# Key loads of 48-KB rows in two places, values two or three chunks behind, in a decode attention kernel

## Chip, cores, metric

One core of a Trainium2 chip; the other cores are idle. The metric is the device time of one execution in microseconds. A "span" is what the profile of one execution covers; it is 1.7 to 1.9 us shorter than the time of that execution in most kernels here (more in three, see e7).

## The reference

One decode step: layer norm of one row, attention with 32 heads over a cache of 32768 keys and values of 192 numbers each, output projection, residual, then a small dense block. Cut to what matters:

```python
B, Sq, D = 1, 1, 640
H, Sk, Dh = 32, 32768, 192
q = (layernorm(x) @ wq).reshape(B, Sq, H, Dh).transpose(0, 2, 1, 3)
scores = jnp.einsum("bhqd,bhkd->bhqk", q, k_cache) * (Dh ** -0.5)
p = softmax(scores, axis=-1)
o = jnp.einsum("bhqk,bhkd->bhqd", p, v_cache)
h = x + o.transpose(0, 2, 1, 3).reshape(B, Sq, H * Dh) @ wo
# ... h2 = h + relu(layernorm(h) @ w1) @ w2
```

Keys and values are 805 MB in bf16, each read once. All inputs together are 825 MB.

## The kernel before

In this kernel each engine has its own program, and semaphores tie them. A head's keys come in four loads of 128 partitions x 64 keys (a row of 24 KB for each partition), its values likewise. A load is worked off in two chunks of 32 keys per partition. In each chunk PE transposes a part of the keys and multiplies it with the query, DVE does the rest by multiply and reduce, ACT takes the exponentials, and PE sums the values with them.

```python
kt = [sbuf(f"kt{i}", [P, JL * Dh], bf16, 512) for i in range(NL)]   # 4 key places of 24 KB
vt = [sbuf(f"vt{i}", [P, JL * Dh], bf16, 512) for i in range(NV)]   # 2 value places of 24 KB
# ... the issuing queue (cut):
for h in range(H):
    for ld in range(NL if h < LAST else NL - 1):
        n = NL * h + ld
        load(kt[ld][:], rows(k_hd, h, P * JL * ld, JL), f"dk{ld}", "k", h, ld)
        if n >= NV:
            hp, lp = divmod(n - NV, NL)
            g.wait("PV", hp, 2 * lp + 1)          # PE has summed what lay in this value place
        load(vt[ld % NV][:], rows(v_hd, h, P * JL * ld, JL), f"dv{ld % NV}", "v", h, ld)
# ... PE, one head (cut):
for c in range(NC):
    transposes(g, h, c)
    if c > 0:
        values(g, h, c - 1)                       # values one chunk behind
    elif h > 0:
        values(g, h - 1, NC - 1)
        den_mm(g, h - 1)
    scores_pe(g, h, c)
```

The end of the last head has its own loads: keys of 40, 16 and 8 per partition, their values, then the two weights of the dense block.

The softmax here doesn't subtract the row's maximum and nothing guards it: scores larger than these inputs give would overflow.

## Time and profile before

| | |
|---|---|
| time, median | 1924.24 us (1924.01 to 1924.29, 3 runs) |
| span of the profiled run | 1922.4 us |
| bytes moved | 825.26 MB in 44793 packets |
| rate in the middle | 432 to 433 GB/s |
| PE, DVE busy | 81%, 81% |

The rows of the page with 40 figures cut the span into 40 slices: busy tenths for an engine, GB/s for the transfers. The chain of waits follows the work that ended last backwards; where it consists of transfers (76% of the span here), they were what the work waited for. A landing time counts from the issue of a load to its last byte: a key load that lands 22.5 us after its issue, three times the 7.28 us of its own transfer, is taken to have had two others ahead of it. The prediction shows these lines.

### The profile page before, as it was taken

The numbers are of one execution on the slowest core, as the hardware profiler recorded it, in microseconds if no ns is written. First come the engines' busy times: TensorE is split into PE (matmuls) and PEld (weight loads), VectorE is DVE, ScalarE is ACT, GpSimd is POOL, SyncE is SP. The second block draws the span as 40 slices with busy tenths as digits, with TensorE's granted clock in tenths as the row PEclk, the third lists the DMA queues.
The fourth block names the chain that finished last, engine by engine and source line by source line (L and its number), as shares of the span: only waits on it lengthen the run. The fifth ranks groups of instructions, "written<-read, shape, count | busy, mean of one in ns | idle before, by whom it ended". The sixth has DMA issues, their size and how long they took to land.

```text
span 1922.4 us, 36522 instructions
## 1 busy us (share of the span) xinstructions
PE 1563.5 (81%) x15899; PEld 1073.1 (56%) x15899; DVE 1560.6 (81%) x734; ACT 970.7 (50%) x2031; POOL 0.7 (0%) x6
## 2 busy tenths in 40 slices
PE   5888888788888888788787888888878887888887
PEld 4555555555555555555555555555545555555555
DVE  5878888887887888787888878888778887888886
ACT  3555455454555555454454555545445454555554
POOL 0000000000000000000000000000000000000000
PEclk9898888988888898888898888888888888898888
DMA  9999999999999999999999999999999999999998
GB/s 405 430 431 432 432 434 433 433 431 432 433 431 433 434 433 432 432 432 428 435 434 433 432 432 433 433 432 432 432 433 433 432 433 433 432 433 433 433 430 342
DMA packets 44793, 825.26 MB, mean 429 GB/s; under 512 B 4580, under 2 KB 6116, under 8 KB 12132
## 3 DMA queue, kind: packets, MB, share of 16 engines
q1 hardware_dynamic: 44762, 824.99, 99.9%
q8 instruction: 12, 0.20, 0.0%
q14 instruction: 9, 0.07, 0.0%
q10 hardware_dynamic: 10, 0.00, 0.0%
HBM read 824.97 MB, written 0.00 MB: 429 GB/s over the span
## 4 chain that ended last, share of the span: by engine, by line
DMA 76%; PE 21%; SPq 2%; issue 1%; ACT 0%; POOLq 0%; DVE 0%
DMA kt<-in_A_k_cache_dram 76%; PE o_ps L324 11%; PE tp L343 10%; SPq L224 2%; PE sp L324 0%; PE attT L324 0%; ACT kT L538 0%; POOLq L306 0%; PE mm L324 0%; DVE o_pair L638 0%; ACT pB L544 0%; PE mm L527 0%; DVE y_row L713 0%; ACT h1T L600 0%; DVE oT L648 0%
## 5 line engine op out<-in xcount | busy, mean ns | idle before, releaser
L623 DVE TENSOR_TENSOR pr<-kt,qb 128x2304 f32<-128x2304 bf16 (+2 forms) x257 | 756.0, 2942 | 278.9 <-POOLq L290 261.5
L538 ACT COPY kT<-tp 128x1024 bf16<-128x1024 bf16 (+1 forms) x899 | 818.8, 992 | 319.3 <-PE tp L343 317.3
L343 PE MATMUL tp<-ident_f,kt 128*128 128x128 f32 x3459 | 569.7, 331 | 334.3 <-POOLq L306 334.3
L626 DVE TENSOR_REDUCE sc<-pr 128x12 f32<-128x2304 f32 (+2 forms) x257 | 755.3, 2939 | 8.9
L343 PEld LDWEIGHTS tp<-ident_f,kt 128*128 128x128 f32 x3459 | 496.1, 172 | 351.3 <-POOLq L306 350.1
L324 PE MATMUL o_ps<-vt,pB 128*2 128x384 bf16 x2286 | 472.5, 358 | 6.8 <-POOLq L306 6.6
L324 PE MATMUL o_ps<-vt,pA 128*2 128x384 bf16 x1778 | 331.0, 326 | 0.0
L324 PEld LDWEIGHTS o_ps<-vt,pB 128*2 128x2 bf16 x2286 | 184.5, 89 | 244.7 <-issue 88.3
L544 ACT ACTIVATE pB<-sp 128x20 bf16<-128x20 f32 (+2 forms) x258 | 47.9, 186 | 504.5 <-PE sp L324 504.5
L324 PEld LDWEIGHTS sp<-qm,kT 128*128 128x128 bf16 x6918 | 193.3, 97 | 77.9 <-issue 65.2
L324 PEld LDWEIGHTS o_ps<-vt,pA 128*2 128x2 bf16 x1778 | 150.7, 85 | 144.9 <-issue 7.9
L324 PE MATMUL sp<-qm,kT 128*128 128x2 bf16 x6918 | 212.0, 164 | 3.1 <-ACT kT L538 2.4
L553 ACT ACTIVATE pA<-sc 128x12 bf16<-128x12 f32 (+2 forms) x257 | 53.4, 208 | 106.4 <-DVEq L65 104.7
L544 ACT ACTIVATION_READ_ACCUMULATOR pB<-sp 128x1 f32 x258 | 50.2, 195 | 0.0
L553 ACT ACTIVATION_READ_ACCUMULATOR pA<-sc 128x1 f32 x257 | 48.7, 190 | 0.0
L631 DVE TENSOR_REDUCE rec<-mm 128x1 f32<-128x20 f32 x32 | 5.7, 179 | 50.3 <-PE mm L324 49.8
L324 PE MATMUL mm<-wq_s,xn_ln 128*1 (+1 forms) x160 | 18.7, 248 | 4.0 <-POOLq L306 4.0
L638 DVE TENSOR_SCALAR o_pair<-o_ps,rec 2x384 bf16<-2x384 f32 x32 | 19.4, 605 | 2.7 <-PE o_ps L324 1.7
L324 PE MATMUL attT<-oT,wo_s 128*128 128x1 bf16 x465 | 15.9, 163 | 0.3 <-DVE oT L648 0.3
L324 PEld LDWEIGHTS mm<-dsums,ones_mat 128*128 128x128 f32 x64 | 9.5, 188 | 10.7 <-issue 9.3
L324 PEld LDWEIGHTS attT<-oT,wo_s 128*128 128x128 bf16 x465 | 13.8, 96 | 0.4 <-DVE oT L648 0.4
L324 PE MATMUL mm<-ones_row,row_e 1*128 1x1 bf16 x384 | 14.0, 159 | 0.0
(71 smaller groups left out, 144.9 us busy)
## 6 DMA issues: line engine op xcount, KB each, us to landing
kt<-in_A_k_cache_dram SPq DMA_DIRECT2D x127, 3072.0 KB, 22.5
vt<-in_A_v_cache_dram SPq DMA_DIRECT2D x127, 3072.0 KB, 15.6
wq_s<-in_A_wq_dram SPq DMA_DIRECT2D x4, 1920.0 KB, 21.0
wo_s<-in_A_wo_dram SPq DMA_DIRECT2D x16, 480.0 KB, 16.3
kt<-in_A_k_cache_dram SPq DMA_DIRECT2D x1, 1920.0 KB, 20.2
kt<-in_A_v_cache_dram SPq DMA_DIRECT2D x2, 960.0 KB, 24.8
kt<-in_B_w_dram SPq DMA_DIRECT2D x1, 1920.0 KB, 18.5
wq_s<-in_B_w_dram SPq DMA_DIRECT2D x1, 960.0 KB, 20.5
```

The lines of the kernel that those rows point to most:

```text
L224: g.do(lambda: nc.sync.dma_start(out=dst, in_=src), sem, label, by=16)
L324: return lambda: pe.matmul(o, lhsT=w, rhs=r, **kw)
L343: calls.append(lambda b=b, o=o: pe.transpose(out=dst[:, b, :], in_=src[:, o:o + 2 * P].bitcast(f32), identity=ident_f[:]))
L538: g.do(lambda: act.copy(out=kT[c % 2][:, b0:b0 + nb, :], in_=src[:, 0:nb, :].bitcast(bf16)), "act_pe", ("cp", h, c, k))
L544: g.do(lambda: act.activation(out=pB[c % 4][:, 0:jp], in_=sp[:, 0:jp], func=F.Exp, scale=SCALE, accum_out=dsums[:, 2 * c + 1:2 * c + 2]), ...
L553: g.do(lambda: act.activation(out=pA[c % 4][:, 0:jd], in_=sc[c % NC][:, 0:jd], func=F.Exp, scale=SCALE, accum_out=dsums[:, 2 * c:2 * c + 1 ...
L623: g.chain(lambda: dve.tensor_tensor(out=pr[:, 0:j1 - j0, :], in0=src[:, (off + j0) * Dh:(off + j1) * Dh].rearrange("p (j d) -> p j d", d=D ...
L626: g.chain(lambda: dve.reduce_sum(out=sc[c % NC][:, j0:j1], in_=pr[:, 0:j1 - j0, :], axis=X), "dve")
L631: g.chain(lambda: dve.reduce_sum(out=rec[:, 0:1], in_=mm[:, 0:2 * NCM], axis=X), "dve")
L638: g.do(lambda: dve.tensor_scalar_mul(out=o_pair[:, :, 1, :], in0=o_ps[0:2, 0:2 * Dh].rearrange("q (i d) -> q i d", i=2), scalar1=rec[0:2, ...
```

## The change

The intent is larger rows: for all heads but the last, two key loads of 128 keys per partition (48-KB rows) into two places, instead of four of 64 into four. Values stay at 24-KB rows. As four chunks can start only when a whole key load is there, values come two or three chunks behind the scores (one in the kernel before), and the order of the loads is key 0, old value 3, value 0, key 1, value 1, value 2. In the last head the keys lead their values. The core of the diff:

```diff
-    kt = [sbuf(f"kt{i}", [P, JL * Dh], bf16, 512) for i in range(NL)]
+    kt = [sbuf(f"kt{i}", [P, JK * Dh], bf16, 512) for i in range(NK)]
...
+        def keys(h, ld):
+            if h > 0:
+                g.wait("PV", h - 1, 4 * ld + 1)
+                g.wait("scs", h - 1, 4 * ld + 3)
+            load(kt[ld][:], rows(k_hd, h, P * JK * ld, JK), f"dk{ld}", "k", h, ld)
+
+        def vals(h, ld):
+            if ld == 1 and h > 0:
+                g.wait("PV", h, 0)
+            elif ld > 1:
+                g.wait("PV", h, 2 * ld - 3)
+            elif h > 0:
+                g.wait("PV", h - 1, 5)
...
+    SUMS = ((), (-2,), (-1,), (0, 1), (), (2,), (3,), (4, 5))
     def pe_head(g, h, turn=None):
         for c in range(NC):
             transposes(g, h, c)
-            if c > 0:
-                values(g, h, c - 1)
...
+            for d in SUMS[c]:
+                if d >= 0:
+                    values(g, h, d)
+                elif h > 0:
+                    values(g, h - 1, NC + d)
             scores_pe(g, h, c)
...
     def pe_end(g):
...
+        transposes(g, h, 6)
+        values(g, h, 3)
+        for c in (7, 8, 9):
             transposes(g, h, c)
+            if c > 7:
+                values(g, h, c - 4)
             scores_pe(g, h, c - 1)
-            if c > E0 + 1:
-                values(g, h, c - 2)
```

More of the change, by code (lines that the diff above doesn't have):

```diff
@@ L106 @@
     FT = Dff // P
+    JK = 128
     JL = 64
@@ L110 @@
     QG = 8
+    NK = Sk // (P * JK)
     NL = Sk // (P * JL)
@@ L114 @@
     LAST = H - 1
-    assert Sk % (P * JL) == 0 and NL == 4 and 2 * Dh == 3 * P and H % QG == 0 and H % 2 == 0 and H >= 4
-    full = [(c // 2, (c % 2) * J, J, JPS[c % 2]) for c in range(NC)]
+    assert Sk % (P * JK) == 0 and NK == 2 and NL == 4 and 2 * Dh == 3 * P and H % QG == 0 and H % 2 == 0 and H >= 4
+    full = [(c // 4, (c % 4) * J, J, JPS[c % 2], c // 2, (c % 2) * J) for c in range(NC)]
     ENDJ = (40, 16, 8)
-    ends = full[:NC - 2] + [(NL - 1, 0, 20, 12), (NL - 1, 20, 20, 12), (NL, 0, 16, 8), (NL + 1, 0, 8, 8)]
+    ends = [(c // 2, (c % 2) * J, J, JPS[c % 2]) for c in range(NC - 2)]
+    ends += [(NL - 1, 0, 20, 12), (NL - 1, 20, 20, 12), (NL, 0, 16, 8), (NL + 1, 0, 8, 8)]
+    ends = [q + q[0:2] for q in ends]
     assert sum(ENDJ) == JL
@@ L195 @@
     wq_v = wq_s[:].rearrange("p (c n) -> p c n", c=DT)
-    k_at = {(LAST, NL - 1): kt[3][:, 0:40 * Dh],
-            (LAST, NL): kt[0][:, 40 * Dh:56 * Dh], (LAST, NL + 1): kt[0][:, 56 * Dh:64 * Dh]}
-    v_at = {(LAST, NL - 1): kt[0][:, 0:40 * Dh],
-            (LAST, NL): kt[1][:, 0:16 * Dh], (LAST, NL + 1): kt[1][:, 16 * Dh:24 * Dh]}
-    w1_s = kt[1][:, 24 * Dh:24 * Dh + DT * Dff].rearrange("p (c n) -> p c n", n=Dff)
+    k_at = {0: kt[0][:, 0:64 * Dh], 1: kt[0][:, 64 * Dh:128 * Dh], 2: kt[1][:, 0:64 * Dh],
+            3: kt[1][:, 64 * Dh:104 * Dh], 4: kt[1][:, 104 * Dh:120 * Dh], 5: kt[1][:, 120 * Dh:128 * Dh]}
+    v_at = {3: kt[0][:, 0:40 * Dh], 4: kt[0][:, 40 * Dh:56 * Dh], 5: kt[0][:, 56 * Dh:64 * Dh]}
+    w1_s = kt[0][:, 64 * Dh:64 * Dh + DT * Dff].rearrange("p (c n) -> p c n", n=Dff)
     w2_s = wq_s[:, 0:FT * D].rearrange("p (f n) -> p f n", n=D)
-    assert 24 * Dh + DT * Dff <= JL * Dh and FT * D <= DT * QG * Dh
+    assert DT * Dff <= JL * Dh and FT * D <= DT * QG * Dh
     W2_CUTS = (0, FT // 2, FT - 2, FT)
     def k_tile(h, ld):
-        return k_at[(h, ld)] if (h, ld) in k_at else kt[ld][:]
+        return k_at[ld] if h == LAST else kt[ld][:]
     def v_tile(h, ld):
-        return v_at[(h, ld)] if (h, ld) in v_at else vt[ld % NV][:]
-    names = ["pool_pe", "act_pe", "dve_pe", "act_dve", "dve_act", "dve", "dve_row", "pe_dve", "pool_row", "pool_dve", "pool_act", "pe_act", "pe"]
-    names += [f"dk{i}" for i in range(NL)] + [f"dv{i}" for i in range(NV)] + ["dwq", "dwo", "dx", "dout"]
-    names += [f"dke{i}" for i in range(2)] + [f"dve{i}" for i in range(4)] + ["dw1"] + [f"dw2_{i}" for i in range(3)]
+        return v_at[ld] if h == LAST and ld in v_at else vt[ld % NV][:]
+    names = ["pool_pe", "act_pe", "dve_pe", "act_dve", "dve_act", "dve", "dve_row", "pe_dve", "pool_row", "pool_dve", "pool_act", "pe_act", "pe", "dve_sp"]
+    names += [f"dk{i}" for i in range(NK)] + [f"dv{i}" for i in range(NV)] + ["dwq", "dwo", "dx", "dout"]
+    names += [f"dke{i}" for i in range(4)] + [f"dve{i}" for i in range(4)] + ["dw1"] + [f"dw2_{i}" for i in range(3)]
     sems = {n: nc.alloc_semaphore(n) for n in names}
@@ L227, in rows @@
             return src[h, k0:k0 + P * jl, :].rearrange("(p j) d -> p (j d)", p=P)
-        load(wq_v, wq_view[:, :, 0:QG * Dh], "dwq", "wq", 0)
-        for h in range(H):
-            for ld in range(NL if h < LAST else NL - 1):
-                n = NL * h + ld
-                load(kt[ld][:], rows(k_hd, h, P * JL * ld, JL), f"dk{ld}", "k", h, ld)
-                if n >= NV:
-                    hp, lp = divmod(n - NV, NL)
-                    g.wait("PV", hp, 2 * lp + 1)
-                load(vt[ld % NV][:], rows(v_hd, h, P * JL * ld, JL), f"dv{ld % NV}", "v", h, ld)
-                if ld == 0 and h % QG == QG - 1 and h + 1 < H:
-                    gq = (h + 1) // QG
-                    g.wait("PV", h - 1, 5)
-                    load(wq_v, wq_view[:, :, gq * QG * Dh:(gq + 1) * QG * Dh], "dwq", "wq", gq)
-                if ld == 3 and h % 2 == 0:
-                    if h > 0:
-                        g.wait("prj", h)
-                    load(wo_s[:], wo_view[h // 2], "dwo", "wo", h // 2)
+        def keys(h, ld):
[3 more added lines that the diff above has]
+            load(kt[ld][:], rows(k_hd, h, P * JK * ld, JK), f"dk{ld}", "k", h, ld)
@@ new lines, in vals @@
+        def vals(h, ld):
[5 more added lines that the diff above has]
+                g.wait("PV", h - 1, 5)
+            if h < LAST:
+                src = rows(v_hd, h, P * JK * (ld // 2), JK)[:, (ld % 2) * JL * Dh:(ld % 2 + 1) * JL * Dh]
+            else:
+                src = rows(v_hd, h, P * JL * ld, JL)
+            load(vt[ld % NV][:], src, f"dv{ld % NV}", "v", h, ld)
@@ new lines, in dma_program @@
+        load(wq_v, wq_view[:, :, 0:QG * Dh], "dwq", "wq", 0)
+        for h in range(LAST):
+            keys(h, 0)
+            if h > 0:
+                vals(h - 1, NL - 1)
+            vals(h, 0)
+            if h % QG == QG - 1:
+                gq = (h + 1) // QG
+                g.wait("PV", h - 1, 3)
+                load(wq_v, wq_view[:, :, gq * QG * Dh:(gq + 1) * QG * Dh], "dwq", "wq", gq)
+            keys(h, 1)
+            vals(h, 1)
+            vals(h, 2)
+            if h % 2 == 0:
+                if h > 0:
+                    g.wait("prj", h)
+                load(wo_s[:], wo_view[h // 2], "dwo", "wo", h // 2)
@@ L247, in dma_program, with end_keys @@
+        def end_keys(i, k0, jl, sem):
+            load(k_at[i], rows(k_hd, LAST, k0, jl), sem, "k", LAST, i)
+        for ld in range(NL - 1):
+            if ld != 1:
+                g.wait("PV", LAST - 1, 2 * ld + 1)
+                g.wait("scs", LAST - 1, 2 * ld + 3)
+            end_keys(ld, P * JL * ld, JL, ("dk0", "dke0", "dk1")[ld])
+            if ld == 0:
+                vals(LAST - 1, NL - 1)
+            else:
+                vals(LAST, ld - 1)
         k0 = P * JL * (NL - 1)
@@ L250, in dma_program @@
             at.append((k0, jl))
-            if i == 0:
-                g.wait("PV", LAST - 1, NC - 1)
-            else:
-                g.wait("PV", LAST, 1)
-            load(k_tile(LAST, NL - 1 + i), rows(k_hd, LAST, k0, jl), f"dk{NL - 1}" if i == 0 else f"dke{i - 1}",
-                 "k", LAST, NL - 1 + i)
+            end_keys(NL - 1 + i, k0, jl, f"dke{1 + i}")
             k0 += P * jl
+        vals(LAST, NL - 2)
         i = 0
         for ld, (k0, jl) in enumerate(at):
-            for c, (l, off, jc, jp) in enumerate(ends):
+            for c, (l, off, jc, *_) in enumerate(ends):
                 if l == NL - 1 + ld:
-                    if ld > 0:
-                        g.wait("PV", LAST, 3)
+                    g.wait("PV", LAST, 1)
                     load(v_tile(LAST, l)[:, off * Dh:(off + jc) * Dh],
@@ L266, in dma_program @@
                     i += 1
+        g.wait("PV", LAST, 3)
         load(w1_s, B_w1.rearrange("(c p) n -> p c n", p=P), "dw1", "w1")
-        g.wait("PV", LAST - 1, 5)
+        g.wait("PV", LAST - 1, 4)
         for i, (c0, c1) in enumerate(zip(W2_CUTS[:-1], W2_CUTS[1:])):
@@ L286, in pool_program, with key @@
         relay(g, "wq", 0)
-        for h in range(H):
-            for ld in range(NL if h < LAST else NL - 1):
-                relay(g, "k", h, ld)
-                g.do(lambda: nc.gpsimd.sem_inc(sems["pool_dve"], 1))
-                book_relay(g, "k", h, ld, sem="pool_dve")
-                relay(g, "v", h, ld)
-                if ld == 0 and h < LAST:
-                    relay(g, "wq", h + 1)
-            if h < LAST:
-                relay(g, "W", h)
+        def key(h, ld):
+            relay(g, "k", h, ld)
+            g.do(lambda: nc.gpsimd.sem_inc(sems["pool_dve"], 1))
+            book_relay(g, "k", h, ld, sem="pool_dve")
+        for h in range(LAST):
+            key(h, 0)
+            if h > 0:
+                relay(g, "v", h - 1, NL - 1)
+            relay(g, "v", h, 0)
+            relay(g, "wq", h + 1)
+            key(h, 1)
+            relay(g, "v", h, 1)
+            relay(g, "v", h, 2)
+            relay(g, "W", h)
+        for ld in range(NL - 1):
+            key(LAST, ld)
+            if ld == 0:
+                relay(g, "v", LAST - 1, NL - 1)
+            else:
+                relay(g, "v", LAST, ld - 1)
+        relay(g, "v", LAST, NL - 2)
     def relay(g, *label):
@@ L326, in transposes @@
     def transposes(g, h, c):
-        ld, off, jc, jp = chunks(h)[c]
+        ld, off, jc, jp = chunks(h)[c][:4]
         src = k_tile(h, ld)
@@ L357, in scores_pe @@
     def scores_pe(g, h, c):
-        ld, off, jc, jp = chunks(h)[c]
+        ld, off, jc, jp = chunks(h)[c][:4]
         g.wait("cp", h, c, len(tiles(jp)) - 1)
@@ L377, in values @@
     def values(g, h, c):
-        ld, off, jc, jp = chunks(h)[c]
+        jc, jp, ld, off = chunks(h)[c][2:]
         jd = jc - jp
@@ L398, in values @@
                               stop=(c == len(chunks(h)) - 1 and i == len(order) - 1), skip_group_check=True))
-        pe_group(g, calls, ("PV", h, c))
+        pe_group(g, calls, ("PV", h, c), "pe_dve" if h < LAST and c == NC - 1 else "pe")
     def den_mm(g, h):
@@ L451, in pe_head @@
             transposes(g, h, c)
-            if c > 0:
-                values(g, h, c - 1)
-            elif h > 0:
-                values(g, h - 1, NC - 1)
+            if c == 0 and h > 0:
                 den_mm(g, h - 1)
+            for d in SUMS[c]:
[3 more added lines that the diff above has]
+                    values(g, h - 1, NC + d)
             scores_pe(g, h, c)
-            if c == 1 and h > 0:
+            if c == 3 and h > 0:
                 o_turn(g, h - 1)
-            if c == 2 and h > 0:
+            if c == 4 and h > 0:
                 project(g, h)
@@ L485, in pe_end @@
         h = LAST
-        E0 = NC - 2
-        for c in range(E0):
+        transposes(g, h, 0)
+        den_mm(g, h - 1)
+        scores_pe(g, h, 0)
+        for c in range(1, NC - 2):
             transposes(g, h, c)
-            if c > 0:
-                values(g, h, c - 1)
-            else:
-                values(g, h - 1, NC - 1)
-                den_mm(g, h - 1)
+            values(g, *((h - 1, NC - 3 + c) if c < 3 else (h, c - 3)))
             scores_pe(g, h, c)
-            if c == 1:
+            if c == 3:
                 o_turn(g, h - 1)
-        transposes(g, h, E0)
-        values(g, h, E0 - 1)
-        for c in range(E0 + 1, NCM):
+        transposes(g, h, 6)
+        values(g, h, 3)
+        for c in (7, 8, 9):
             transposes(g, h, c)
+            if c > 7:
+                values(g, h, c - 4)
             scores_pe(g, h, c - 1)
-            if c > E0 + 1:
-                values(g, h, c - 2)
-        scores_pe(g, h, NCM - 1)
+        values(g, h, 6)
+        scores_pe(g, h, 9)
+        values(g, h, 7)
         den_mm(g, h)
-        values(g, h, NCM - 2)
-        values(g, h, NCM - 1)
+        values(g, h, 8)
+        values(g, h, 9)
         o_turn(g, h)
@@ L532, in copies @@
     def copies(g, h, c):
-        ld, off, jc, jp = chunks(h)[c]
+        ld, off, jc, jp = chunks(h)[c][:4]
         t0 = sum(len(tiles(q[3])) for q in chunks(h)[:c])
@@ L547, in exp_dve @@
     def exp_dve(g, h, c):
-        ld, off, jc, jp = chunks(h)[c]
+        ld, off, jc, jp = chunks(h)[c][:4]
         jd = jc - jp
@@ L606, in scores_dve @@
     def scores_dve(g, h, c):
-        ld, off, jc, jp = chunks(h)[c]
+        ld, off, jc, jp = chunks(h)[c][:4]
         jd = jc - jp
@@ L634, in o_scale @@
     def o_scale(g, h):
-        if h == LAST:
-            g.wait("PV", h, NCM - 1)
+        g.wait("PV", h, len(chunks(h)) - 1)
         g.wait("rec", h)
@@ L680, in dve_head @@
             scores_dve(g, h, c)
+            if c % 4 == 3 and h < LAST:
+                g.tell("dve_sp", ("scs", h, c))
             if c == 0 and h > 0:
                 den_rec(g, h - 1)
+            if c == 2 and h > 0:
                 o_scale(g, h - 1)
-            if c == 1 and h > 0:
+            if c == 3 and h > 0:
                 o_turned(g, h - 1)
```

## The prediction

Its sum: 1924.2 - 2.4 (packets) + 0.1 (end) = 1921.9, from which it said 1921.5. Its "fit" is the line through the durations of four packet sizes in the trace of before. In that trace its 2.7 and 3.7 us for a values group go with a granted clock of 1.00 (from 1890 to 1895 us) and 0.58 (from 1885 to 1890). The rivals' causes and sizes (a disliked pitch, a gap of 1 us, 0.5% of rate, 0.1 us for a load's end) are suppositions, not measurements.

> **What bounds the kernel now.** I read the page's slices first, then its chain, then the waits of the DMA queue, then one head by windows, then the end of the chain in order of time.
>
> The page's slices and DMA total:
>
> ```profile
> PE   5888888788888888788787888888878887888887
> DVE  5878888887887888787888878888778887888886
> DMA  9999999999999999999999999999999999999998
> GB/s 405 430 431 432 432 434 433 433 431 432 433 431 433 434 433 432 432 432 428 435 434 433 432 432 433 433 432 432 432 433 433 432 433 433 432 433 433 433 430 342
> DMA packets 44793, 825.26 MB, mean 429 GB/s; under 512 B 4580, under 2 KB 6116, under 8 KB 12132
> ```
>
> PE and DVE are at eight tenths throughout, the 16 DMA engines at nine or more, and the rate is flat at 432 to 433. Only the first slice (start) and the last (end) are lower. 825 MB at 432.3 GB/s is 1909 us of a span of 1922.4, so all but some 13 us is transfer.
>
> The chain, and the DMA queue's own waits:
>
> ```profile
> DMA 76%; PE 21%; SPq 2%; issue 1%; ACT 0%; POOLq 0%; DVE 0%
> ```
>
> ```profile
> SPq L224 <- PE o_ps L324: 1772.9, 126, 33.6
> ```
>
> ```profile
> kt<-in_A_k_cache_dram SPq DMA_DIRECT2D x127, 3072.0 KB, 22.5
> vt<-in_A_v_cache_dram SPq DMA_DIRECT2D x127, 3072.0 KB, 15.6
> ```
>
> The 21% of PE in the chain and the 1772.9 us for which the issuing queue waits for PE could suggest that PE's release of value places holds the transfers up. The landing times deny it. One 3072-KB load takes 3.1457 MB / 432.3 GB/s = 7.28 us (T below), yet a key load lands 22.5 us, three T, after its issue, and a value load two T after. Two other loads lie ahead of each key load: the issuer waits because it is early, and the engines never run dry.
>
> One head of 58.1 us, by windows:
>
> ```profile
> 60.50:118.60 58.10, 48.37 (x493) 33.34 (x493) 48.68 (x22) 30.14 (x63) 0.00 (x0) 0.89 1.01 431
> ```
>
> The columns are PE, weight load, DVE, ACT and POOL busy, the clock, the DMA share and GB/s. For one of a head's eight chunks PE needs 48.37/8 = 6.05 us, DVE 48.68/8 = 6.09, the transfer of its key and value half-loads 7.26.
>
> The end of the chain in order of time:
>
> ```profile
> 1860.46 23.21 DMA kt<-in_A_k_cache_dram
> ...
> 1883.76 3.46 PE tp L343 x15
> 1887.22 3.70 PE o_ps L324 x16
> ...
> 1909.54 2.06 PE o_ps L324 x12
> ...
> 1914.34 1.67 PE o_ps L324 x60
> ...
> 1916.36 1.76 PE attT L324 x60
> ...
> 1918.77 0.28 DVE y_row L713
> ```
>
> After the last whole key load (landed 1883.7) PE works almost without a gap to the end: the last 38.7 us are PE's and not the transfers'. The packet records say that the last weight packet ended at 1914.95, before its use (1916.36 and after).
>
> [...] the packet records last 149 ns for 3840 B, 291 for 7680, 573 for 15360 and 912 for 24576, a line of slope 36.8 ns per 1000 B (27.2 GB/s for one engine, 435 for 16) that starts near 7.7 ns. From start to start on one engine it is 908 ns for 24576 B and some 146 for 3840, so some 4 ns of it is really lost per packet. [...] here loads queue behind one another, and the records show that a load's end costs only 6 ns more (914 from start to start where the completion's 4-byte packet lies between). [...] no trace here has a 48-KB pitch yet.
>
> **The change, part by part.**
>
> 1. *Key rows of 48 KB.* Of 31 heads, 8 loads of 128 x 24 KB become 2 of 128 x 48 KB and 4 of 128 x 24 KB. I take a row as one packet, as it is now (254 loads x 128 rows = 32512, the number of 24576-B packets). Per engine 31 x 2 x 8 = 496 pairs of packets become one each: 496 x 4 ns = 2.0 us. 62 loads fewer end: 62 x 6 ns = 0.4 us. Bytes are the same. Together 2.4 us; taken with the whole 7.7 and 9 ns of the records it would be 4.4, the most that I can derive.
>
> 2. *The values' source.* They keep 24-KB rows, now every 48 KB of the HBM: same packets, no term.
>
> 3. *Chunks start in fours.* A key place of 48 KB must land whole (2 T = 14.6 us), then four chunks can run: 4 x 6.09 = 24.4 us by DVE, 24.2 by PE. The next half-head's keys land after 4 T = 29.1, so compute still waits for keys, 4.7 us a half-head instead of 1.2 a chunk. No engine becomes the bound.
>
> 4. *Places and the issue order* (key 0, old value 3, value 0, key 1, values 1 and 2). Counting from the landing of a head's key 0 at 0, the transfers run: old value 3 in 0 to 1 T, value 0 to 2 T, key 1 to 4 T, value 1 to 5 T, value 2 to 6 T, next key 0 to 8 T. Chunks 0 to 3 end near 3.4 T, chunks 4 to 7 near 7.4 T. So next key 0 may be issued at 3.4 T and is due at 6 T; next key 1 at 7.4 T, due 10 T; value 1 (after the first half of values in chunk 3) near 3 T, due 4 T; value 2 near 3.3 T, due 5 T. The two output-weight and query-weight waits lie similarly. The smallest slack is 1 T, 7 us; in the first head, which starts late, about 5, and in the last two 0.7 T. All are well over an issue's cost (0.3 to 0.5 us in the trace). The engines stay fed: no term. The one new semaphore, from DVE to the issuer, is waited for with that slack.
>
> 5. *The end.* Now the last head's keys land one 24-KB load earlier, and values follow. From the last whole key load there are four T of transfers (value 1, key ends, value 2, value ends) before the final weights instead of three. PE's order from there, with durations of this trace: transposes, values 1, scores, and the same for chunk 5, end near 12 us; then transposes, values 3, transposes, scores, transposes to 18. Then PE must wait for value 2, which lands at 3 T = 21.8. Behind it: 2.7 (values 4), 0.6, 0.8, 2.7 (values 5), 0.4, 1.7 (values 6), 0.4, 1.7 (values 7), 0.4, 2.1 (the last two) = 13.5, so PE's values end near 35.3, as against 1911.6 - 1883.7 = 27.9 now. The way from there to the end stays 1922.4 - 1911.6 = 10.8. So 46.1 instead of 38.7 after that landing; the landing is itself T = 7.3 earlier. Sum: +0.1 us. The last values still miss little, since the final weights (some 10 us of small packets) land near 39.4 and are used from 38 and 40 on.
>
> Sum: 1924.2 - 2.4 + 0.1 = 1921.9; with the upper estimate of the packet term 1919.9. I say 1921.5.
>
> **The rivals.**
>
> *A starved queue.* Keys in two places are coarser: if the release came late, all 16 engines would stand. For it: two places instead of four, 31 x 2 key loads each waiting for both PE and DVE, and values up to three chunks behind. Against it: the slack in step 4, and PE and DVE at 83% of a head. A gap of 1 us for each key load would cost 62 us (1986, slower by 3%). I give it 3%.
>
> *48-KB rows move at another rate.* Slower, if the HBM dislikes the pitch or if a row this long is cut badly: 0.5% of half the bytes is 5 us, against the gain. If rows are cut into two pieces of 24 KB the packet term falls and 1924 remains. Faster than some 4 us cannot follow from the packets, since the fit's slope alone is 435 GB/s: 825 MB at 435 is 1897, plus the same 13 us outside transfer is 1910, and 2% faster is 1886. I leave 2% for it.
>
> *The end goes otherwise.* If PE doesn't wait for value 2 or has a lower clock there, or if the last weights become the bound, the end moves by up to 3 us either way: PE's values matmuls took 2.7 or 3.7 for a group of 16 by the state of the clock.
>
> *A real gain from larger transfers at a load's end.* If one load's end cost 0.1 us of transfer instead of 6 ns, 62 fewer would bring 6 us (1918). The flat 432 speaks against it.
>
> **Range and chances.** The packet term is 0 to 4.4, the end -3 to +3, the rate of the new pitch unknown by perhaps 0.1%: 1917.5 to 1925 for 8 in 10. Faster by over 2%: 0.02. Within 2%: 0.95. Slower by over 2%: 0.03, all of it the starved queue or the pitch.
>
> **What would show it.** Right: the rate of the middle slices at 432.5 to 433.5, the DMA row at nines, some 7900 data packets fewer (496 x 16) and 1000 completions fewer (62 x 16); 49152-B packets of some 1812 to 1816 ns; key loads landing two or more loads after their issue; PE and DVE waiting for keys in fewer, longer stretches; the time from the last whole key load to the end near 46. Wrong: slices that dip below 425, or key loads that land in about 14.6 us, one load alone, which is an empty queue ahead of them; 24576-B packets still 32512; or a middle rate above 435.

## The result

| | before | after |
|---|---|---|
| time, median | 1924.12 us (1923.79 to 1924.29, 4 runs) | 1924.17 us (1923.68 to 1925.44, 4 runs) |
| span of the profiled run | 1922.4 us | 1923.6 us (the slowest of its four) |

The ratio is 1.0001, 95% interval 0.9984 to 1.0019. A ratio here is the mean time of one kernel's fast runs over that of the other's of the same rounds, so it is not quite the ratio of the medians. The time is the same, within the predicted range; the gain of 2.7 us that the prediction had at its middle isn't there.

Page of the changed kernel, slices and DMA total:

```profile
DMA  9999999999999999999999999999999999999997
GB/s 408 433 428 434 435 430 440 429 430 435 429 435 437 426 436 432 432 437 429 438 430 429 438 429 433 439 428 433 431 433 435 430 433 436 431 437 432 430 410 328
DMA packets 35864, 825.25 MB, mean 429 GB/s; under 512 B 3588, under 2 KB 5124, under 8 KB 11140
```

The slices scatter more, because the page counts a packet where it starts and packets are longer: with each packet counted by its share, slices 2 to 38 lie between 430 and 433 (before: 430 and 433 too). What carries is their mean: from 200 to 1800 us the packet records give 432.96 GB/s, each packet counted by its share of that window, against 432.32 before. There are 8929 packets fewer; 7936 of data and 992 completions were foreseen. Slice 39, at 410, has no counterpart before (430 there). PE's share of the chain of waits rose from 21% to 35%, yet the rate in the middle did not fall: as in the prediction, that share doesn't say what sets the time.

The landing times, and how a stretch near the end looks by windows (PE, weight load, DVE, ACT, POOL busy, clock, DMA share, GB/s):

```profile
vt<-in_A_v_cache_dram SPq DMA_DIRECT2D x127, 3072.0 KB, 18.8
kt<-in_A_k_cache_dram SPq DMA_DIRECT2D x62, 6144.0 KB, 32.4
```

```profile
1865.00:1870.00 5.00, 4.45 (x48) 3.15 (x49) 4.85 (x3) 3.72 (x8) 0.00 (x0) 0.70 1.01 431
1870.00:1875.00 5.00, 4.29 (x53) 3.01 (x52) 4.70 (x5) 0.90 (x6) 0.00 (x0) 0.96 0.73 246
1875.00:1880.00 5.00, 5.00 (x61) 3.40 (x60) 4.86 (x4) 3.47 (x6) 0.00 (x0) 1.00 0.94 405
```

Key loads take 14.5 us of transfer and land 32.4 us after their issue, so the queue is well filled in general. But once, from 1870 to 1875, the rate falls to 246 GB/s: the engines ran dry. The DMA queue's own instructions there, and the end of the chain (start, duration, what):

```profile
1848.12 0.43 SPq L227 DMA_DIRECT2D kt<-in_A_k_cache_dram  x1
1872.17 0.33 SPq L227 DMA_DIRECT2D vt<-in_A_v_cache_dram  x1
1872.54 1.72 SPq L227 DMA_DIRECT2D kt<-in_A_k_cache_dram  x3
1878.36 0.33 SPq L227 DMA_DIRECT2D vt<-in_A_v_cache_dram  x1
```

```profile
1848.12 25.57 DMA kt<-in_A_k_cache_dram
...
1878.36 19.60 DMA vt<-in_A_v_cache_dram
...
1898.05 4.26 PE o_ps L368 x16
1902.31 0.54 PE sp L368 x18
...
1910.79 2.06 PE o_ps L368 x12
...
1919.99 0.28 DVE y_row L764
```

The last whole key load landed at 1848.12 + 25.57 = 1873.7. Value load 1 of the last head was issued only at 1872.17, as PE summed the last head's first values until 1872.07. The engines are not in step, so the early ones were dry by then: the packet records show a mean of 13.0 engines at work from 1870 to 1872 and 7.1 from 1872 to 1874, which is ((16 - 13.0) + (16 - 7.1)) x 2 / 16 = 1.5 us of all engines. Later PE waits for value load 2 until 1898.0, and the first values group behind that wait takes 4.26 us instead of 2.69.

The packet records, from the start of a packet to the start of the next one on the same engine (each start is assigned to the engine whose packet had just ended):

```
bytes   before   after   e2 (below)
12288      -        -      456 ns
24576    908 ns   908 ns   908 ns
49152      -     1812 ns     -
between two packets with a completion in between: 6 ns more in all three
```

### The profile page after: what moved, and what is told of

It is laid out like the page before. It is cut to its first block, busy times and chain, and to the rows that moved or that the text cites. A ratio compares the mean times of both kernels' runs of the same rounds, so it can differ in the third digit from the quotient of the medians.

```text
span 1923.6 us, 36300 instructions
## 1 busy us (share of the span) xinstructions
PE 1554.4 (81%) x15899; PEld 1088.3 (57%) x15899; DVE 1560.5 (81%) x734; ACT 966.9 (50%) x2031; POOL 0.7 (0%) x6
## 4 chain that ended last, share of the span: by engine, by line
DMA 55%; PE 35%; ACT 6%; DVE 3%; SPq 1%; issue 0%; POOLq 0%; DVEq 0%
DMA kt<-in_A_k_cache_dram 54%; PE o_ps L368 19%; PE tp L387 10%; ACT kT L587 6%; PE sp L368 4%; PE mm L368 2%; DVE pr L672 1%; DVE sc L675 1%; DMA vt<-in_A_v_cache_dram 1%; PE attT L368 1%; SPq L227 1%; ACT pA L602 0%; POOLq L350 0%; DVE o_pair L686 0%; ACT row_e L607 0%
## 5 line engine op out<-in xcount | busy, mean ns | idle before, releaser
L672 DVE TENSOR_TENSOR pr<-kt,qb 128x2304 f32<-128x2304 bf16 (+2 forms) x257 | 755.9, 2941 | 303.9 <-POOLq L321 278.7
L387 PE MATMUL tp<-ident_f,kt 128*128 128x128 f32 x3459 | 578.1, 334 | 240.8 <-POOLq L350 238.6
L387 PEld LDWEIGHTS tp<-ident_f,kt 128*128 128x128 f32 x3459 | 501.8, 174 | 252.4 <-POOLq L350 244.0
L368 PE MATMUL o_ps<-vt,pB 128*2 128x384 bf16 x2286 | 459.2, 351 | 7.9 <-POOLq L350 7.1
L368 PEld LDWEIGHTS mm<-dsums,ones_mat 128*128 128x128 f32 x64 | 15.1, 291 | 0.3 <-issue 0.3
L368 PEld LDWEIGHTS attT<-oT,wo_s 128*128 128x128 bf16 x465 | 14.5, 101 | 0.4 <-DVE oT L696 0.4
## 6 DMA issues: line engine op xcount, KB each, us to landing
kt<-in_A_k_cache_dram SPq DMA_DIRECT2D x62, 6144.0 KB, 32.4
```

The costliest lines, as they stand in the source:

```text
L368: return lambda: pe.matmul(o, lhsT=w, rhs=r, **kw)
L387: calls.append(lambda b=b, o=o: pe.transpose(out=dst[:, b, :], in_=src[:, o:o + 2 * P].bitcast(f32), identity=ident_f[:]))
L672: g.chain(lambda: dve.tensor_tensor(out=pr[:, 0:j1 - j0, :], in0=src[:, (off + j0) * Dh:(off + j1) * Dh].rearrange("p (j d) -> p j d", d=D ...
```

## The experiments

All times of this section come in two groups: e1, e3, e4 and e5 on one chip, the others on another. The kernel before took 1924.2 to 1924.34 (medians) on both. The intervals of the ratios are some 0.13% either way, 2.5 us: against the kernel before, only e1, e2 and e7 are clear of 1. What is smaller is read from medians, from whether the executions overlap, and from the traces. Two theories were to be told apart. *Theory A*: the long rows gave what the packets promise, 2.4 us, and the new end took it back. *Theory B*: the long rows gave nothing, and the slightly higher rate is chance or due to the order.

### e1, two key loads: only the rows undone

```diff
-            load(kt[ld][:], rows(k_hd, h, P * JK * ld, JK), f"dk{ld}", "k", h, ld)
+            for i in range(2):
+                w = JK * Dh // 2
+                load(kt[ld][:, i * w:(i + 1) * w], rows(k_hd, h, P * JK * ld, JK)[:, i * w:(i + 1) * w],
+                     f"dk{ld}", "k", h, ld)
```

> The changed kernel with each 48-KB key row fetched as two loads of 24-KB rows; order, places and waits stay. Packet theory (4 ns less for each merged pair, 6 ns less for each load end): 7936 packets of 49152 B turn into 15872 of 24576 B, start to start 908 ns instead of 1812, so the middle rate falls from 432.7 back to about 432.2 GB/s and the last whole key load lands about 2.4 us later in its span. In the whole time this is +1 to +2.5 us, at the edge of what rounds resolve. Rival (the longer rows gave nothing, and the higher middle rate is chance or comes from the new order): the middle rate stays at 432.7 and the time is unchanged.

Measured: 1927.31 us median (1926.52 to 1928.28, 5 runs), ratio to before 1.0017 (1.0003 to 1.003). The records have 24576-B packets alone for whole loads, at 908 ns, and 432.32 GB/s from 200 to 1800 us, the rate of before. Page of e1:

```profile
DMA packets 44792, 825.25 MB, mean 429 GB/s; under 512 B 4580, under 2 KB 6116, under 8 KB 12132
```

That is the packet count of before, in the new order. The whole rest of the change without the rows is thus 3.0 us slower than the kernel before, and the rows make that up. Theory B would have had the time of the changed kernel. The difference to it is 2.5 us (a0's 1924.8) to 3.1 (1924.17), at or over the upper end of the expected 1 to 2.5.

### e2, four key loads: the slope

The same edit with 4 pieces of 12 KB.

> The changed kernel with each 48-KB key row fetched as four loads of 12-KB rows: against two loads of 24 KB twice as many ends and splits again, which gives the packet term a slope. Packet theory: per engine 3 x 496 more packets of 4 ns = 6.0 us and 3 x 62 more load ends of 6 ns = 1.1 us, together 7.1 us against the changed kernel: 12288-B packets 456 ns from start to start, middle rate about 431.1 GB/s, time about 1931. Rival (row length gives nothing, the two-load run was slower for its order or by chance): time as with two loads or as the changed kernel, 1924 to 1927.

Measured: 1932.88 us (1932.35 to 1933.31), ratio 1.0044 (1.003 to 1.0058); beside it the changed kernel itself at 1924.8 (a0 below). 8.1 us, where 7.1 were expected. A 12288-B packet takes 456 ns from start to start, as expected, so that a split costs 4 ns at this length too (2 x 456 - 908), and the rate from 200 to 1800 us is 431.05 GB/s. Page of e2:

```profile
DMA packets 62649, 825.27 MB, mean 427 GB/s; under 512 B 6564, under 2 KB 8100, under 8 KB 14116
```

So with 8, 16 and 32 key packets per load and engine the time is 1924.2 to 1924.8, 1927.3 and 1932.9. Theory B falls. Of the 1.0 us that is over, most may lie near the start: from 20 to 200 us e2 has 428.4 GB/s, 0.6% under its later 431.0 (the changed kernel, a0, 431.9, 0.25% under its own 433.0), which is 0.7 us of 180. Why is open.

### a0, the changed kernel again

> The changed kernel itself again, as the measure for the other three of this chip. All theories: within 0.1% of the kernel before, about 1924.2, with the dip of the transfers between 1870 and 1875 again and the middle rate at 432.7.

Measured: 1924.8 us (1923.78 to 1927.8), ratio 1.0005 (0.9991 to 1.0019). One expectation failed: the dip isn't there. Windows of a0:

```profile
1870.00:1875.00 5.00, 0.81 (x9) 0.72 (x9) 4.09 (x5) 0.57 (x4) 0.00 (x0) 0.95 0.98 408
1895.00:1898.00 3.00, 1.81 (x6) 0.72 (x7) 2.60 (x2) 0.00 (x0) 0.00 (x0) 0.50 0.99 416
1898.00:1901.00 3.00, 3.00 (x11) 1.13 (x9) 0.00 (x0) 0.00 (x0) 0.00 (x0) 0.50 1.01 415
```

In this execution value load 1 was issued at 1869.30, just in time, and value load 2 landed at 1896.1, 21.8 us after the last whole key load. The dip belongs to some executions only. Yet the time is no better, because PE's clock stood at 0.50 for two whole windows behind the wait, and the first values group took 5.3 us.

### e3, value load 1 early: only the dip taken away

The last values group of the head before now signals the semaphore that the issuing queue can read, and value load 1 of the last head waits for that one. The result of the run is correct.

```diff
-            if ld == 1 and h > 0:
+            if ld == 1 and h == LAST:
+                g.wait("PV", h - 1, NC - 1)
+            elif ld == 1 and h > 0:
                 g.wait("PV", h, 0)
...
-... ("PV", h, c), "pe_dve" if h < LAST and c == NC - 1 else "pe")
+... ("PV", h, c), "pe_dve" if h < LAST - 1 and c == NC - 1 else "pe")
```

> The changed kernel, where the last head's value load 1 waits only for the last use of its place (the last values group of the head before, at 1864.4 in the profile) and not for the first values group of the last head (1872.1). Theory that the queue ran dry once: the dip to 246 GB/s in 1870 to 1875 is gone, the load's issue comes some 7 us earlier, transfers end 1.5 us earlier, and the whole time falls by about 1.5 us. Rival (the end is PE's alone, the dip costs nothing): dip gone, time unchanged within 0.5 us.

Measured: 1923.7 us (1923.65 to 1924.7), ratio to before 0.9999 (0.9985 to 1.0012). The load went out at 1864.62, and the dip is gone:

```profile
1870.00:1875.00 5.00, 1.41 (x18) 1.31 (x16) 4.63 (x5) 0.58 (x4) 0.00 (x0) 0.70 0.99 428
```

The profiled span is 1921.9, 1.7 under that of the changed kernel; of the medians 0.5 to 1.1 us remains, less than the expected 1.5, and the interval doesn't tell it from zero. That fits a dip which only some executions have; it is not shown that the dip cost time. In this trace, too, the clock was at half behind PE's wait, from 1895.9 to 1899.3.

### e4 and e5, scores before the last values

In the last head PE does the transposes and scores of chunks 7 to 9 before it waits for value load 2; 8 instead of 4 small buffers for the exponentials make that legal. e5 adds the edit of e3.

```diff
         for c in (7, 8, 9):
             transposes(g, h, c)
-            if c > 7:
-                values(g, h, c - 4)
             scores_pe(g, h, c - 1)
-        values(g, h, 6)
         scores_pe(g, h, 9)
-        values(g, h, 7)
+        for c in (4, 5, 6, 7):
+            values(g, h, c)
```

> The changed kernel, where PE in the last head does the transposes and scores of chunks 7 to 9 before it waits for value load 2 (with 8 instead of 4 small buffers for the exponentials so that this is legal). Theory that the end is PE's work behind value load 2's landing (14.8 us in the profile, of which about 2.0 us are scores and transposes, and more at a low clock): that work falls to about 11 to 12.5 us, and the time by 2 to 3 us, until the last weights' landing bounds the end. Rival (the end is bound by the last weights or by DVE and ACT): time unchanged within 0.5 us.

> Both edits of the two runs before. If each gives what is expected alone, the time falls by 3.5 to 4.5 us against the changed kernel, to about 1920, and the end is then bound by the transfer of the last weights: the last product group starts within 1 us after the last weight packet. If the last weights bind sooner, 2.5 to 3.5 us.

Measured: e4 1923.15 us (1920.51 to 1925.45), ratio 0.9993 (0.9979 to 1.0007); e5 1922.53 us (1920.53 to 1924.85), ratio 0.999 (0.9977 to 1.0004). Both missed most of what was expected, and their executions differ by 4 to 5 us. The profiled execution of e5 was its slowest (1924.85), and its chain tells what held that one:

```profile
1896.63 1.39 ACT kT L587 x2
1898.25 0.48 PE sp L370 x12
1898.73 11.04 PE o_ps L370 x52
1909.77 0.33 PE mm L370 x2
```

The scores of chunk 9 wait for ACT's chain of copies and exponentials until 1898.2, 2.1 us after value load 2 landed (1896.1). And 52 matmuls take 11.04 us; at 168 ns each (16 in 2.69 us at full clock) they would take 8.7. The granted clock in e5 is 0.5 from 1896.9 to 1903.8. So in this execution the order puts one wait in the place of another, and the clock falls again. Why others of the same kernel took 1920.5 no trace shows. e4's profiled run has the dip too.

### e8, needless matmuls in the wait: the clock by itself

```diff
             transposes(g, h, c)
+            if c == 8:
+                fill(g, 40)     # 40 matmuls of 2 x 128 into columns of the bank that nothing reads
             if c > 7:
                 values(g, h, c - 4)
```

> The changed kernel with 40 needless matmuls on PE (into unused columns) just where it waits for value load 2 in the last head. Theory that this wait drops the clock to half, so that the values behind it take 4.26 us instead of 2.69: the granted clock stays at 1.0 from 1890 to 1905, the group takes about 2.7 us, the time falls by about 1.5 us. Rival (the half clock comes from elsewhere, or the matmuls delay the group themselves): clock 0.5 after the wait as before, time unchanged or longer.

Measured: 1922.67 us (1922.02 to 1923.38), ratio to before 0.9991 (0.9978 to 1.0005), 2.1 us under a0 on the same chip; all five executions are under the fastest of a0 (1923.78). A window and a group of the changed kernel, for comparison:

```profile
1898.00:1901.00 3.00, 2.95 (x10) 1.23 (x11) 0.99 (x1) 0.00 (x0) 0.00 (x0) 0.50 1.01 425
```

```profile
1898.05 3.29 PE L368 MATMUL o_ps<-vt,pB 128*2 128x384 bf16 x10 [2.53 <-POOLq L350]
```

Windows of e8 and PE's instructions in order of time:

```profile
1895.00:1898.00 3.00, 2.84 (x42) 2.30 (x40) 2.97 (x2) 2.04 (x8) 0.00 (x0) 1.00 0.96 406
1898.00:1901.00 3.00, 3.00 (x37) 1.92 (x34) 0.16 (x1) 0.44 (x4) 0.00 (x0) 1.00 1.00 412
```

```profile
1894.67 2.39 PE L368 MATMUL o_ps<-ident_b 128*2 128x128 bf16 x40
1897.23 1.79 PE L368 MATMUL o_ps<-vt,pB 128*2 128x384 bf16 x10 [0.16 <-POOLq L350]
```

The clock stays at 1.00, and ten matmuls that took 3.29 us in the changed kernel take 1.79. This profiled run has the dip (280 GB/s from 1870 to 1875) and still a span of 1921.4. The half clock behind a wait is a cause by itself.

### e7 and e10, the mended end

e3's early load, e4's buffers, scores 8 and 9 between the values, and 10 needless matmuls before the scores of chunk 7 and before the values of chunk 4.

```diff
...
+        transposes(g, h, 7)
+        scores_pe(g, h, 6)
+        transposes(g, h, 8)
+        fill(g, 10)
+        scores_pe(g, h, 7)
+        transposes(g, h, 9)
+        fill(g, 10)
+        values(g, h, 4)
+        scores_pe(g, h, 8)
+        values(g, h, 5)
+        scores_pe(g, h, 9)
+        values(g, h, 6)
+        values(g, h, 7)
```

> Value load 1 issued early, scores of chunks 6 and 7 before value load 2 lands but 8 and 9 between the values, 8 small buffers, and 2 x 10 needless matmuls in PE's short waits. If queue and end are both understood, value load 2 lands near 1895.8, PE's values end near 1908 to 1909.5 (1912.8 in the changed kernel), the last weights near 1912.8 become the bound, and the time is about 1920 to 1921, 3 to 4 us under the changed kernel. Rival (PE's clock or ACT's chain still bound the end): 1922 to 1924.

> The version with the mended end once more, on another set of rounds: about 1921.3, 3 us under the kernel before.

Measured: e7 1921.35 us (1920.97 to 1921.79), ratio to before 0.9985 (0.9971 to 0.9999); e10 1921.62 us (1920.73 to 1924.05), ratio 0.9988 (0.9974 to 1.0001). The end of e7's chain:

```profile
1905.67 2.06 PE o_ps L370 x12
...
1912.54 1.77 PE attT L370 x60
...
1914.96 0.28 DVE y_row L775
```

PE's values end at 1907.7, and the last product with weights starts at 1912.54 while the last weight packet ends near 1912.8: transfers and PE now end together. e7 is the fastest version, about 3 us or 0.15% under both kernels, where 1920 to 1921 had been expected. One thing is left open: the times of e7, e9 and e10 exceed their spans by 1.8 to 3.0 us, those of the other kernels by 1.7 to 1.9, so only part of the shorter span (1918.6) shows in the time.

### e9, the mended end with short rows

> The mended end, but each 48-KB key row as two loads of 24-KB rows. If the longer rows' 2.4 us are worth their whole size once nothing at the end gives them back: 2 to 3 us slower than the mended version, about 1923.5 to 1924, the kernel before's own time. Rival (the mended end alone made the gain, the rows nothing): the same time as the mended version within 0.7 us.

Measured: 1923.79 us (1923.5 to 1924.77, 6 runs), ratio to before 0.9999 (0.9986 to 1.0011), beside e10 at 1921.62. The difference of 2.2 us is the packet term, now seen in the time: all six executions took 1923.5 or more, nine of the ten of e7 and e10 at most 1921.8.

### The end in one table

Us from the span's start, from the chains of the profiled runs. "Key" is the landing of the last whole key load, "value 2" that of value load 2 of the last head.

| run | key | value 2 after key | PE's values end after value 2 | span |
|---|---|---|---|---|
| before | 1883.7 | - | (27.9 after key) | 1922.4 |
| prediction for after | 1874.0 | 21.8 | 13.5 | 1920.1 |
| after | 1873.7 | 24.3 | 14.9 | 1923.6 |
| a0 | 1874.3 | 21.8 | 15.9 | 1922.9 |
| e1 | 1876.9 | 21.8 | 15.1 | 1924.7 |
| e3 | 1873.9 | 21.8 | 15.1 | 1921.9 |
| e8 | 1873.7 | 23.4 | 13.4 | 1921.4 |
| e7 | 1873.9 | 21.8 | 12.0 | 1918.6 |

(The row of the prediction: 1883.7 - 7.3 - 2.4, and its 46.1 us to the end.)

## Why the prediction was right, and which term was not

- *What bounds the kernel.* Right: PE and DVE stayed at 81%, the rate stayed flat, and no engine became the bound in the middle. What rate is possible at most was not shown. The slope of the prediction's fit, 36.8 ns per 1000 B, is 435 GB/s for 16 engines, an estimate from packet durations; the 432 to 433 measured here, with the other cores idle, lie within 0.7% of it.
- *Step 1, packets.* Right: one packet for a 48-KB row, 1812 ns, 4 ns less than two of 908; 496 x 4 ns + 62 x 6 ns = 2.4 us. The last whole key load landed 10.0 us earlier, 7.3 by order and 2.4 by packets foreseen. e1, e2 and e9 show the term in the time: 2.2 to 3.1 us for one split, 8.1 for three. The larger value of 4.4 is refuted.
- *Step 2, the values' source.* Right: a 24576-B packet takes 908 ns at either pitch (24 KB before, 48 KB after).
- *Step 3, chunks in fours.* Right. The page of the changed kernel has 61 waits of DVE for keys instead of 102, with 278.7 us in total instead of 261.5: fewer and longer.
- *Step 4, the slack.* Right for 31 heads: from 60 to 1850 us the records show 0.4 us of idle for an engine, as before the change (0.4). Too large in the last head, where the smallest slack was put at 0.7 T (5 us): that places value load 1's release at 1873.7 - 0.7 x 7.3 = 1868.6 on this trace's scale, and it came at 1872.1. PE began the head at 1848.5 (a0: 1847.2), and the group that releases the place ran from 1868.4 to 1872.1, partly at half clock (0.70 granted from 1865 to 1870 us); a0, at full clock there (1.00), had it from 1866.5 to 1869.2. The rival of a starved queue thus happened once, 1.0 to 1.5 us long, in some executions (the traces of the changed kernel, e4 and e8, not a0's). e3 removes the dip. In e1 the same release came at 1871.3 and no engine ran dry, as its last whole key load landed 3.2 us later than the changed kernel's: the faster rows themselves took up a part of the slack.
- *Step 5, the end.* This is the mis-sized term: "+0.1 us" was +3.9 in the profiled run, 49.9 us from key to end (1923.6 - 1873.7) instead of 46.1. Of the 3.8 between, 2.5 is value load 2's later landing, which e1, e3 and a0 do not have, and 1.4 is PE's work behind it, which all three have (1.6 to 2.4). The profiled run was the slowest of the four; the median of their spans, 1922.3, would make it some +2.6, an estimate that takes this landing for all four. The prediction gave 2.7 us to the first values group behind the wait; it took 4.26, and 5.3 in a0, as the clock falls to half in that wait (0.50 granted from 1898 to 1901 us in both). It named "a lower clock there" among the rivals, but held the 2.7 for the middle. With the clock held up (1.00 from 1895 to 1904 us in e8) the work behind value 2 is 13.4, as worked out.
- Sum: -2.4 of packets stands. In the time the rest of the change costs +3.0 (e1), not +0.1, and so the median came out at 0.0 instead of -2.7. The range held because it left the end 3 us either way, not because the sum was right.

On the clock: in the changed kernel it was at half from 1897.7 to 1901.1, 3.4 us, and in a0 for two such windows. What the traces show before such a fall is little work of PE, not always none. The clock changes of a trace lie on a grid of 3.413 us. The window before the fall in the changed kernel, 1894.31 to 1897.72, still held 1.21 us of PE's work, and that in e5, 1893.53 to 1896.94, 2.20 us. Over eleven traces (all but e2's), of 4310 such windows at full clock from 30 to 1905 us, each with less than 1.4 us of PE's work was followed by half clock and none with more than 2.5; between these it went either way. What the border depends on besides this work no run tests.

## What to carry to other kernels

Here transfers ran at 432 to 433 GB/s, of 435 by the estimate from the packet fit, and longer rows saved only the few nanoseconds between packets: 4 ns for each pair merged and 6 ns for each load end less, 2.2 to 3.1 us of 1924 (e9, e1). So count packets and multiply before restructuring, and work out what the order that longer rows force costs (here 3.0 us, more than the 2.4 us reckoned for the rows). Work out the last few loads on their own, with the slower durations of a PE at half clock: behind a wait of 2.5 us there, 16 matmuls took 4.26 us instead of 2.69, some 1.5 us on top of the wait. Reckon the slack of an issue from when the first of the 16 engines runs dry, not from the landing: here an issue 1.5 to 2.2 us before the landing of the load ahead left engines dry, one 5.0 us before it (a0) did not.
